# Setting the sign of the weight words with a 16-bit one-tensor operation

## The chip, the cores and the metric

The kernel runs on one core of one Trainium2 chip. The metric is the device time of one execution in microseconds; of the kernel before, three runs are given. The core's engines are TensorE (PE in the rows, its weight loads PEld), VectorE (DVE), ScalarE (ACT), GpSimd (POOL) and SyncE (SP, which issues the transfers). Each works off its own queue in order, and an instruction waits on semaphores for work of the others.

## The reference

A linear attention with an exponential feature map feeds a feed-forward layer with a squared ReLU:

```python
def phi(x):                      # q, k, v: (8, 8, 576, 64); w_phi: (64, 128)
    proj = np.einsum('bhsd,df->bhsf', x, w_phi)
    proj = proj - np.max(np.abs(proj), axis=-1, keepdims=True)
    return np.concatenate([np.exp(proj), np.exp(-proj)], axis=-1)
q_p, k_p = phi(q), phi(k)
kv, z = np.einsum('bhsf,bhsd->bhfd', k_p, v), np.sum(k_p, axis=2)
num = np.einsum('bhsf,bhfd->bhsd', q_p, kv)
x = num / (np.einsum('bhsf,bhf->bhs', q_p, z)[..., None] + 1e-06)   # to (4608, 512)
h = np.maximum(x @ w_in, 0.0)                                       # w_in: (512, 2048)
out = (h * h) @ w_out                                               # w_out: (2048, 512)
```

The two weights `w_in` and `w_out` of the feed-forward layer reach the kernel as 64-bit floats, the other inputs as 32-bit floats.

## The kernel before

**Stages.** The attention is done in 32 pairs of heads, the feed-forward layer in 18 chunks of 256 tokens by 8 blocks of 256 hidden columns. The first 6 pairs are done by the function `early`, and the weights are prepared beside them; from about 98 us on the matrix products of the feed-forward layer (lines 1180 and 1222) fill PE, with the later pairs in between.

**The weights.** Each of the two weights is cut into 8 parts of 128 x 1024 numbers; `raw0i` to `raw7i` are the parts of `w_in` and `raw0o` to `raw7o` those of `w_out`. A part comes in as 128 x 2048 32-bit words, in which low and high word of a 64-bit float alternate, so that every access to the low words or the high words has a step of 8 bytes. The function `join_words` makes 32-bit floats of them in four steps: `size` (lines 489 and 491) scales the high word, read as a 32-bit float, which brings exponent and upper fraction bits into a tile `u`; `low` (497 on ACT, 499 on DVE) rounds the low word to a number of 0 to 7 and writes it over the low word; `ends` (502, DVE) ands the sign bit out of the high word and ors it into the low word; `join` (506, DVE) shifts `u` by 3 bits and ors the low word in. Of the 16 `low` steps 13 stand on ACT and 3 on DVE. What follows on a part of `w_in` is its largest size (523), a scale (442 to 447, from PE's line 436) and the 16-bit halves `win` (565, 566, 568); on a part of `w_out` the high part `wh` (542, 544) and the rest `wl` (327, on POOL in the rows below).

**What else the prediction names.** For a pair, lines 739, 742, 749 and 752 on DVE and 745 to 757 on ACT turn the key features into exponentials; 852 and 854 do the subtraction for the queries, and 886 and 888 their exponentials; 896 on PE is the numerator. The denominator goes from PE (913) by ACT (334, tile `sx`) to a transfer (921, `den`), DVE (930, 931), a transfer to memory (934, `rd`), two transfers back that spread it over the partitions (941, `rb`), and the product on DVE (948). Line 601 and line 586 belong to the scale of the values `v`.

**What sets the order.** Each step is recorded with an estimate, its dependences and a rank; a planner puts the steps of all engines in order by a table of ranks, chooses the engine for steps that may run on two (`other=`), and the instructions are then issued in that order on each engine.

Of the kernel before, what the change touches and what calls it, by code (L numbers as in the profile page):

```python
# [16 lines left out]
BF16 = mybir.dt.bfloat16  # L17
I32 = mybir.dt.int32
U32 = mybir.dt.uint32
AF = mybir.ActivationFunctionType  # L20
ALU = mybir.AluOpType
AX = mybir.AxisListType
# [44 lines left out]
def word(x):  # L67
    return x - (1 << 32) if x >= 1 << 31 else x
# [218 lines left out]
def out_us(n):  # L287

    return 0.165 + n / 1200


def dve_us(n):
    return (n + 151) / 960
# [20 lines left out]
def tile_kernel(ctx, tc, qp, kp, vp, w_phi, w_in, w_out, out):  # L314
    nc = tc.nc
    V, A, G, PE, SP = nc.vector, nc.scalar, nc.gpsimd, nc.tensor, nc.sync
# [12 lines left out]
    def copy(n, to, of, by=None):  # L329

        if by:
            return (("ACT", out_us(n) + 0.09, lambda: A.activation(out=to(), in_=of(), func=AF.Copy, scale=by())),  # L332
                    ("DVE", dve_us(n), lambda: V.tensor_scalar(out=to(), in0=of(), scalar1=by(), scalar2=None, op0=ALU.mult), None))
        return (("ACT", out_us(n), lambda: A.activation(out=to(), in_=of(), func=AF.Copy)),
                ("DVE", dve_us(n), lambda: V.tensor_copy(out=to(), in_=of()), None))
# [129 lines left out]
    def fetch(n, f, of_in, rank):  # L465
        home = home_of[f, of_in]
        box = []
        src = w_in if of_in else w_out

        def load():  # L470
            box.append(cp.tile([128, 2048], I32, name=f"raw{f}{'io'[not of_in]}", tag=home))
            SP.dma_start(box[0], src[f])

        ld = P.add("SP", 0.47, load, [home_read[home]] if home in home_read else [], [], rank - 3.0 + 0.3 * n,
                   land=2.4, xfer=2.55)
        return ld, lambda: box[0][:, 0:2048:2], lambda: box[0][:, 1:2048:2]

    def join_words(n, f, of_in, rank):

        home = home_of[f, of_in]  # L480
        key = [("u", n)]
        u = lambda: u_[0][n]
        ld, low_w, high_w = fetch(n, f, of_in, rank)
        if of_in:
            spare[f] = low_w

        def size(E):
            if E is A:
                A.activation(out=u().bitcast(F32), in_=high_w().bitcast(F32), func=AF.Copy, scale=2.0 ** -111)
            else:  # L490
                V.tensor_scalar(out=u().bitcast(F32), in0=high_w().bitcast(F32), scalar1=2.0 ** -111, scalar2=None,
                                op0=ALU.mult)

        def low(E):
            to, of, a, b = low_w(), low_w().bitcast(U32), 0.875 * 2.0 ** -29, 0.4995
            if E is A:
                A.activation(out=to, in_=of, func=AF.Copy, scale=a, bias=b)
            else:
                E.tensor_scalar(out=to, in0=of, scalar1=a, scalar2=b, op0=ALU.mult, op1=ALU.add)

        def ends():
            V.scalar_tensor_tensor(out=low_w(), in0=high_w(), scalar=word(0x80000000), in1=low_w(),
                                   op0=ALU.bitwise_and, op1=ALU.bitwise_or)

        def join():
            V.scalar_tensor_tensor(out=u(), in0=u(), scalar=3, in1=low_w(),
                                   op0=ALU.logical_shift_left, op1=ALU.bitwise_or)

        sz = P.add("ACT", 1.15, lambda: size(A), [ld], key, rank, other=("DVE", 0.64, lambda: size(V), 4.0))
        l = P.add("ACT", 1.15, lambda: low(A), [ld], [], rank, other=("DVE", 0.68, lambda: low(V), 4.0))  # L510
        o = P.add("DVE", 1.22, ends, [l], [], rank, lock=4.0)
        o = home_read[home] = P.add("DVE", 1.22, join, [sz, o], key, rank, lock=4.0)
        return o

    def value(n, t):
        return u_[0][n].bitcast(F32).rearrange("p (t c) -> p t c", t=t)

    def split_in(n, f, rank):
        o = join_words(n, f, True, rank)
        g, i = divmod(f, 2)  # L520

        def most():
            A.activation(out=spare[f]().bitcast(F32), in_=u_[0][n].bitcast(F32), func=AF.Abs, accum_out=wmax[g][:, i:i + 1])

        most_in[f] = home_read[home_of[f, True]] = P.add("ACT", 1.06, most, [o], [("u", n)], rank)
        return o
# [9 lines left out]
    def out_high(n, f, rank, joined):  # L536
        j = slice(2 * (f % 2), 2 * (f % 2) + 2)

        def high(E):
            x = highs[f] = part(highs_of, f, F32R, "wh")[:, j]  # L540
            if E is A:
                A.activation(out=x, in_=value(n, 2), func=AF.Copy)
            else:
# [1018 lines left out]
    for n, (f, of_in) in enumerate(order_w):  # L1562
        rank = PREP0 + PREP1 * n
        if of_in:
            half[f] = n, rank, split_in(n, f, rank)
            if f % 2:
                pw = power(lambda g=f // 2: wmax[g], cw[:, f - 1:f + 1, :], TOP_W, [most_in[f - 1], most_in[f]], [],
                           half[f - 1][1], k=2)
                for x in (f - 1, f):
                    w_done[x, True] = value_in(x, *half[x], pw)  # L1570
        else:
            half_out[f] = n, f, rank, out_high(n, f, rank, join_words(n, f, False, rank))
            for x in {NFP - 2: (), NFP - 1: (f - 1, f)}.get(f, (f,)):
                w_done[x, False] = out_low(*half_out[x])
# [3 lines left out]
    for p in range(NPAIR):  # L1578
        if p % NP == 0 and p:
            b = p // NP  # L1580
# [127 lines left out]
```

## Time and profile before

| what | us |
|---|---|
| median of 3 runs (lowest, highest) | 1026.27 (1025.84, 1026.85) |
| the profiled execution, its own time | 1027.7 |
| its span, first to last instruction | 1025.9 |
| around the span | 1.8 |
| PE busy | 995.9 (97%) |
| DVE busy | 851.5 (83%) |
| ACT busy | 766.2 (75%) |
| POOL busy | 168.4 (16%) |

The span is the time from the first to the last instruction. Shares of busy time are means over stages that differ: at the start PE waits, later it hardly does. Numbers in brackets at the end of a timeline row are the engine's idle time before that group and what ended it.

### The profile page before, as it was taken

How to read it: one execution, taken by the hardware profiler on the slowest of the kernel's cores; microseconds unless marked ns; L12 is line 12 of the kernel's file. 1: busy time of each engine (PE TensorE's matmuls, PEld its weight loads, DVE VectorE, ACT ScalarE, POOL GpSimd, SP SyncE). 2: the span in 40 equal slices, each digit the busy share in tenths (PEclk: the TensorE clock that was granted, in tenths of full speed). 3: DMA queues.
4: the chain of work that ended last, by engine and by line, in shares of the span. 5: the costliest groups of instructions: out<-in, count | busy, mean ns of one | idle time of the engine just before them, and what ended most of it. 6: DMA issues, size and time to landing. Idle time of an engine off the chain costs nothing.

```text
span 1025.9 us, 21473 instructions
## 1 busy us (share of the span) xinstructions
PE 995.9 (97%) x8353; PEld 693.8 (68%) x8370; DVE 851.5 (83%) x1664; ACT 766.2 (75%) x1426; POOL 168.4 (16%) x114
## 2 busy tenths in 40 slices
PE   7887999999999999999999999999999999999998
PEld 4555676666666666566666566666666667888886
DVE  6899888898999997998888786888798899756453
ACT  7898886877989777887889667858785767654553
POOL 0013143303112112121112103102211110000000
PEclk9998999999999999999999999999999999999999
DMA  9644421221322222322323232132212111000000
GB/s 360 251 154 140 146 61 58 73 69 50 83 62 67 51 60 77 92 55 61 105 62 81 75 83 56 43 88 61 61 43 56 20 46 33 1 2 26 17 22 22
DMA packets 92937, 76.30 MB, mean 74 GB/s; under 512 B 61476, under 2 KB 70308, under 8 KB 90788
## 3 DMA queue, kind: packets, MB, share of 16 engines
q1 hardware_dynamic: 92836, 74.93, 24.8%
q8 instruction: 66, 1.08, 0.4%
q14 instruction: 35, 0.29, 0.1%
HBM read 61.18 MB, written 13.68 MB: 73 GB/s over the span
## 4 chain that ended last, share of the span: by engine, by line
PE 80%; DVE 7%; DMA 5%; ACT 4%; issue 2%; SPq 1%; POOL 0%; DVEq 0%; ACTq 0%; POOLq 0%
PE ph L1180 34%; PE po L1222 25%; PE pv L779 4%; PE pp L1495 3%; PE pn L1000 2%; DMA raw3o<-in_w_out_dram 2%; PE po L1495 2%; PE pv L1000 2%; PE pp L709 1%; PE pn L1495 1%; PE pv L1495 1%; PE pp L1076 1%; PE pv L784 1%; DMA raw0i<-in_w_in_dram 1%; DMA rb<-rd 1%
## 5 line engine op out<-in xcount | busy, mean ns | idle before, releaser
L1180 PE MATMUL ph<-ring,win 128*128 128x256 f16 x3456 | 392.5, 273 | 1.2 <-DVE gl L327 1.2
L1180 PEld LDWEIGHTS <-win 128*128 128x128 f16 x3456 | 334.9, 98 | 61.3 <-issue 13.3
L1222 PE MATMUL po<-wl,gh 128*128 128x512 f16 (+1 forms) x767 | 185.4, 379 | 1.4 <-issue 0.8
L1099 POOL PARTITION_ALL_REDUCE mx<-pt x52 | 116.3, 2237 | 426.7 <-ACT pt L332 274.5
L1222 PEld LDWEIGHTS <-gh 128*128 128x128 f16 (+1 forms) x784 | 75.0, 98 | 83.3 <-issue 5.1
L327 DVE TENSOR_TENSOR gl<-ph,gh 128x512 f16<-128x512 f32 (+1 forms) x114 | 77.5, 680 | 21.9 <-ACT ph L1201 15.1
L1222 PE MATMUL po<-wl,gl 128*128 128x512 f16 x328 | 84.3, 379 | 0.0
L1197 ACT ACTIVATE r<-ph,cwr 128x512 f32<-128x512 f32 x82 | 55.8, 682 | 36.8 <-PE ph L1180 36.3
L1222 PEld LDWEIGHTS <-gl 128*128 128x128 f16 (+1 forms) x456 | 41.9, 98 | 55.8 <-issue 7.4
L1199 ACT ACTIVATE gh<-r 128x512 f16<-128x512 f32 (+1 forms) x114 | 71.3, 625 | 5.1 <-PE pv L1495 3.0
L779 PE MATMUL pv<-e,v 128*64 128x256 f32 x512 | 64.7, 389 | 6.0 <-ACT e L747 4.2
L327 DVE TENSOR_TENSOR v<-qe,gh 128x896 f16<-128x896 f32 x30 | 32.8, 1092 | 42.3 <-ACT gh L1483 42.0
L1201 ACT ACTIVATE ph<-r 128x512 f32<-128x512 f32 x114 | 67.2, 590 | 0.3
L779 PEld LDWEIGHTS pv<-e,v 128*64 128x64 f32 x512 | 36.3, 140 | 23.9 <-ACT e L747 6.1
L1104 ACT ACTIVATE qe<-qe 128x576 f32<-128x576 f32 x52 | 35.3, 679 | 20.1 <-DVE qe L327 19.7
L327 DVE TENSOR_TENSOR qe<-pt,mx 128x576 f32<-128x576 f32 x52 | 39.7, 764 | 10.4 <-POOL mx L1099 10.3
L1115 DVE SCALAR_TENSOR_TENSOR pt<-qe,zc,pt 128x576 f32<-128x576 f32 x52 | 41.9, 810 | 5.4 <-ACT pt L1111 5.2
L1483 ACT ACTIVATE gh<-qe 128x896 f16<-128x896 f32 x30 | 28.4, 946 | 24.0 <-PE pv L1495 8.8
L1495 PEld LDWEIGHTS <-gh 128*128 128x128 f16 x420 | 41.1, 98 | 4.7
L1468 ACT ACTIVATE r<-ph,cwr 128x512 f32<-128x512 f32 x30 | 20.6, 686 | 29.4 <-PE ph L1180 29.3
L1477 DVE TENSOR_TENSOR qe<-qe 128x256 f32<-128x256 f32 (+1 forms) x90 | 28.8, 375 | 15.9 <-ACT qe L1473 15.8
L745 ACT ACTIVATE e<-e,sc 128x512 f32<-128x512 f32 x48 | 34.2, 716 | 9.0 <-DVE e L742 8.7
(369 smaller groups left out, 1983.1 us busy)
## 6 DMA issues: line engine op xcount, KB each, us to landing
v<-in_vp_dram SPq DMA_DIRECT2D x32, 320.0 KB
k<-in_kp_dram SPq DMA_DIRECT2D x32, 288.0 KB
q<-in_qp_dram SPq DMA_DIRECT2D x32, 288.0 KB
rb<-rd SPq DMA_DIRECT2D x64, 144.0 KB
out_dram<-o SPq DMA_DIRECT2D x28, 256.0 KB
td<-kvs SPq DMA_DIRECT2D x26, 128.0 KB
kz<-td SPq DMA_DIRECT2D x104, 32.0 KB
zq<-zd SPq DMA_DIRECT2D x104, 2.0 KB
```

The costliest lines, as they stand in the source:

```text
L327: eng.tensor_tensor(out=out_, in0=a, in1=b_, op=ALU.subtract)
L779: PE.matmul(out=to[64 * h:64 * h + 64, 0:256], lhsT=v_[p][:, t, h, :], rhs=e_[2 * p + h][:, t].rearrange("p s f -> p (s f)"), start=t == 0 ...
L1000: PE.matmul(out=to[64 * h:64 * h + 64, :], lhsT=kz_[n][:, 128 * s_ + 64 * h:128 * s_ + 64 * h + 64], rhs=qe_[2 * n + h].rearrange("p (s x) ...
L1099: o = P.add("POOL", par_us(S), lambda n=n, h=h: G.partition_all_reduce(mx_[n], pt_[p][:, h, :], channels=128, reduce_op=bass_isa.ReduceOp. ...
L1104: o = P.add("ACT", act_us(S), lambda qe=qe: A.activation(out=qe(1), in_=qe(0), func=AF.Exp, scale=-1.0), [o], [("qe", n)], R(RQ + 0.4))
L1115: o = P.add("DVE", dve_us(S) + 0.05, lambda h=h, qe=qe, y=y: V.scalar_tensor_tensor(out=y(), in0=qe(1), scalar=zc_[p][:, 2 * h + 1:2 * h + ...
L1180: PE.matmul(out=ph[:, j, :], lhsT=win[w][:, t, 128 * ff:128 * ff + 128], rhs=ring[half][x][:, t, c0:c0 + T], start=k == 0, stop=k == 3 * K ...
L1197: o = P.add("ACT", act_us(512, 1), lambda: A.activation(out=r_[n], in_=ph_[bank], func=AF.Relu, scale=by()), [g1] + wait, [("ph", bank), ( ...
L1199: sq = P.add("ACT", act_us(512), lambda: A.activation(out=gh(), in_=r_[n], func=AF.Square), [o], [("r", n), ("gh", n)], Q)
L1201: o = P.add("ACT", 0.59, lambda: A.activation(out=ph_[bank], in_=r_[n], func=AF.Square), [o], [("ph", bank), ("r", n)], Q, other=("DVE", 0 ...
L1222: PE.matmul(out=po_[po[i][1]], lhsT=g[:, j, 128 * i:128 * i + 128], rhs=w[:, j, :], start=(f == (NFP - ENDS if last else 0) and (s, j) == ...
L1495: PE.matmul(out=to, lhsT=l()[:, a], rhs=r(slice(b_, b_ + 1))[:, 0], start=(f == 0 and k == 0 and place % 2 == 0), stop=(f == NFP - 1 - END ...
```

## The change

`ends` becomes an operation on one tensor. It no longer reads the low word: it reads the upper 16 bits of the high word, ands them with 0x8000 and writes the result to the upper 16 bits of the low word. So that this leaves a clean word, `low` writes its number of 0 to 7 as a 16-bit integer to the lower 16 bits of the low word alone; it still reads all 32 bits. Both 16-bit accesses have a step of 8 bytes, as the 32-bit ones had. `join` reads the same 32-bit word as before.

```diff
+U16 = mybir.dt.uint16
...
+        halves = lambda x: x().bitcast(U16)
+
         def low(E):
-            to, of, a, b = low_w(), low_w().bitcast(U32), 0.875 * 2.0 ** -29, 0.4995
+            to, of, a, b = halves(low_w)[:, :, 0], low_w().bitcast(U32), 0.875 * 2.0 ** -29, 0.4995
             if E is A:
                 A.activation(out=to, in_=of, func=AF.Copy, scale=a, bias=b)
             else:
                 E.tensor_scalar(out=to, in0=of, scalar1=a, scalar2=b, op0=ALU.mult, op1=ALU.add)
 
         def ends():
-            V.scalar_tensor_tensor(out=low_w(), in0=high_w(), scalar=word(0x80000000), in1=low_w(),
-                                   op0=ALU.bitwise_and, op1=ALU.bitwise_or)
+            V.tensor_scalar(out=halves(low_w)[:, :, 1], in0=halves(high_w)[:, :, 1], scalar1=0x8000, scalar2=None,
+                            op0=ALU.bitwise_and)
```

The planner's estimates, ranks and dependences are untouched. On every engine the same instructions stand in the same order as before; 16 of them on DVE are of another kind (TENSOR_SCALAR in place of SCALAR_TENSOR_TENSOR), and 16 `low` instructions have another output. `ends` still waits for `low` of its part. Two parts, `raw5i` and `raw4o`, swap the buffers of `u` that they get, so that of the two `size` instructions on ACT that stand next to each other (at 80.3 and 81.3 us) the second now waits for POOL's `wl` and the first for DVE, where it was the other way round; and the load of `raw6o` waits, besides what it waited for, for ACT's `low` of the part that lay in its buffer before.

## Rows read from the trace of the kernel before

**Rows 1.** The page's parts 1 and 2: the span, busy time by engine, and the granted TensorE clock in 40 equal slices (in tenths of full speed).

```profile
span 1025.9 us, 21473 instructions
...
PE 995.9 (97%) x8353; PEld 693.8 (68%) x8370; DVE 851.5 (83%) x1664; ACT 766.2 (75%) x1426; POOL 168.4 (16%) x114
...
PEclk9998999999999999999999999999999999999999
```

**Rows 2.** Busy time by stretch of the span. Columns: stretch, its length, busy us (and instructions) of PE, PEld, DVE, ACT and POOL, granted clock, share of the transfer engines, GB/s.

```profile
58.00:69.00 11.00, 9.47 (x121) 5.83 (x120) 10.77 (x16) 10.68 (x21) 2.38 (x1) 1.00 0.63 230
69.00:82.00 13.00, 8.48 (x111) 5.69 (x105) 12.59 (x20) 12.35 (x19) 3.17 (x1) 0.91 0.33 96
82.00:98.00 16.00, 13.27 (x125) 8.13 (x125) 13.55 (x20) 12.45 (x22) 5.04 (x2) 0.75 0.52 179
98.00:140.00 42.00, 40.96 (x344) 29.23 (x339) 36.63 (x63) 35.42 (x60) 7.28 (x3) 1.00 0.34 113
140.00:1026.00 886.00, 877.13 (x7178) 614.18 (x7191) 732.57 (x1461) 648.12 (x1221) 147.48 (x101) 1.00 0.21 55
```

**Rows 3.** What PE waited for from 98 us to the end: us in total, times, longest us. The three largest.

```profile
PE pp L1076 <- DVE e L742: 1.4, 2, 1.0
PE ph L1180 <- DVE gl L327: 1.2, 1, 1.2
PE pp L877 <- ACT qe L888: 0.9, 1, 0.9
```

**Rows 4.** The instructions of line 502 (`ends`, the first and the last of 16) and of line 499 (`low` on DVE, the first and the last of 3): ns min/median/max, first and last start in us, shape.

```profile
L502 DVE SCALAR_TENSOR_TENSOR raw0i<-raw0i x1: 1210/1210/1210, 17.6 to 17.6; 128x1024 int32<-128x1024 int32 x1
...
L502 DVE SCALAR_TENSOR_TENSOR raw7o<-raw7o x1: 1216/1216/1216, 132.7 to 132.7; 128x1024 int32<-128x1024 int32 x1
...
L499 DVE TENSOR_SCALAR raw0i<-raw0i x1: 687/687/687, 14.4 to 14.4; 128x1024 int32<-128x1024 uint32 x1
...
L499 DVE TENSOR_SCALAR raw7i<-raw7i x1: 705/705/705, 117.4 to 117.4; 128x1024 int32<-128x1024 uint32 x1
```

**Rows 5.** Timelines up to 47 us: ACT (its step before the transfer `den`, and the step that waits for it), SP's issue of that transfer, and two waits of DVE. Columns: start us, us, engine, line, operation, out<-in, shape, count, and in brackets the idle time before.

```profile
32.51 0.53 ACT L334 ACTIVATE sx<-pn 128x288 f32<-128x288 f32 x1
...
39.67 0.74 ACT L586 ACTIVATE sx<-v 128x640 bf16<-128x640 f32 x1 [3.49 <-DMA den<-sx]
...
33.34 0.70 SPq L921 DMA_DIRECT2D den<-sx  x1
...
43.83 1.23 DVE L502 SCALAR_TENSOR_TENSOR raw0o<-raw0o 128x1024 int32<-128x1024 int32 x1 [1.64 <-ACT raw0o L497]
...
46.27 0.29 DVE L852 TENSOR_REDUCE qm<-pn 128x1 f32<-128x128 f32 x1 [0.61 <-PE pn L847]
```

**Rows 6.** Timelines of 68 to 82 us, with the columns of rows 5: ACT, PE, DVE, POOL and SP, in this order.

```profile
68.00 1.22 ACT L497 ACTIVATE raw2o<-raw2o 128x1024 int32<-128x1024 uint32 x1
...
72.40 2.19 ACT L565 ACTIVATE win<-u,cw 128x1024 f16<-128x1024 f32 x2
...
70.17 0.71 PE L436 MATMUL pn<-ident,wm 128*128 128x128 f32 x4
...
81.26 2.19 PE L896 MATMUL pn<-qe,kz 128*64 128x288 f32 x8 [1.30 <-DVE pt L854]
...
69.24 1.23 DVE L502 SCALAR_TENSOR_TENSOR raw2o<-raw2o 128x1024 int32<-128x1024 int32 x1 [0.48 <-ACT raw2o L497]
...
70.99 0.41 DVE L442 TENSOR_REDUCE pw<-pn 128x2 f32<-128x256 f32 x1
...
72.84 1.19 DVE L502 SCALAR_TENSOR_TENSOR raw4o<-raw4o 128x1024 int32<-128x1024 int32 x1
...
75.09 1.27 DVE L568 SCALAR_TENSOR_TENSOR win<-u,cw,win 128x1024 f16<-128x1024 f32 x1
...
76.48 1.27 DVE L568 SCALAR_TENSOR_TENSOR win<-u,cw,win 128x1024 f16<-128x1024 f32 x1
77.68 2.36 DVE L930 TENSOR_SCALAR den<-den 128x9 f32<-128x9 f32 x1
...
80.20 0.71 DVE L948 TENSOR_TENSOR rb<-n,rb 128x576 f32<-128x576 f32 x1
80.83 0.28 DVE L854 TENSOR_TENSOR pt<-pn,qm 128x128 f32<-128x128 f32 x1
...
76.83 3.17 POOL L327 TENSOR_TENSOR wl<-u,wh 128x1024 bf16<-128x1024 f32 x1 [9.16 <-ACT wh L542]
...
76.14 1.30 SPq L941 DMA_DIRECT2D rb<-rd  x2
```

**Rows 7.** The chain of waits, a piece of an earlier pair: start us, us from issue to landing of the second of its two `rb` transfers.

```profile
52.92 4.48 DMA rb<-rd
```

**Rows 8.** Busy time by stretch, with the columns of rows 2, around PE's half-speed stretches.

```profile
79.50:80.00 0.50, 0.45 (x8) 0.20 (x4) 0.50 (x1) 0.50 (x2) 0.50 (x1) 0.72 0.00 0
80.00:81.20 1.20, 0.00 (x0) 0.00 (x0) 1.17 (x5) 1.20 (x3) 0.01 (x1) 0.50 0.03 2
81.20:85.80 4.60, 4.54 (x20) 2.49 (x20) 3.57 (x5) 4.28 (x9) 0.00 (x0) 0.50 0.24 70
85.80:89.40 3.60, 0.88 (x8) 0.58 (x8) 3.57 (x6) 3.15 (x8) 0.00 (x0) 0.90 0.37 98
90.00:93.40 3.40, 3.40 (x22) 2.01 (x22) 3.38 (x3) 2.52 (x5) 2.66 (x1) 0.50 0.71 267
```

## The prediction, made before the changed kernel was run

> **What bounds the kernel now.** I read the page's busy times and clock first. PE is busy for 995.9 of 1025.9 us, and the granted clock is at or near full speed in all 40 slices but one tenth in the first [rows 1]. Of the 30 us in which PE is not busy most must lie early, so I cut the span into stretches [rows 2]. From 98 us on PE is busy for 40.96 of 42.00 and then for 877.13 of 886.00 us at a granted clock of 1.00. Before that it is not: 9.47 of 11, 8.48 of 13, 13.27 of 16, at granted clocks of 1.00, 0.91 and 0.75. There DVE and ACT are both nearly full (10.77 and 10.68 of 11, 12.59 and 12.35 of 13). So the end is set by how early the preparation lets PE's solid run begin, and after 98 us almost by PE alone: its three largest sums of waits come to 1.4 + 1.2 + 0.9 = 3.5 us, and none of them names a weight word of `ends` or `low` [rows 3]. Only then did I read timelines, at each place where DVE or ACT had been waiting, to see whose end came last there [rows 5, 6].
>
> **What the change removes.** An `ends` takes 1.210 us at first and 1.216 at last; the nearest one-tensor operation of DVE, on the same 1024 numbers with the same step of 8 bytes, is `low`, with 0.687 and 0.705 [rows 4]. I take 0.68 for the new `ends`, a gain of 0.53 each, 16 x 0.53 = 8.5 us of DVE. The bounds: 1.21, no gain, if the engine gives the 16-bit access no more than two tensors get; and, on the low side, half of the 0.69, if a 16-bit element goes at twice the pace of a 32-bit one.
>
> The Trainium skill ("VectorE: DVE Perf Modes", "What auto-detection actually checks") has a rule for this: twofold speed for one source in SBUF with fitting dimensions, and fourfold only if every tensor is also 16-bit with step 1. The step here is 4 elements, so by the page `ends` would get the twofold speed, as the `low` of rows 4 seems to (0.69 against 1.21), and not the fourfold; by fourfold the sum below would hardly change, because it is not the size of the gain that limits it.
>
> `low` keeps its instruction and writes 2 bytes instead of 4. On ACT it takes 1.22 us (at 68.00), and the two `win` instructions, which write 16 bits, take 2.19 / 2 = 1.10 each for as many numbers [rows 6]. So I take no change, with bounds of -0.1 and, upward, the 0.6 of a rival below. The order stays on all engines; the swapped `u` buffers and the added wait of a load I cost at nothing, because ACT's two `size` instructions stand next to each other, and a load is asked for long after its buffer's `low`. If that cover were gone, ACT would stand up to one step of about 1.2 us.
>
> **Where the gain goes.** I follow 0.53 us down each stretch.
> - The early parts, up to 39.67 us: ACT runs without a gap to its step `sx` at 32.51, which ends at 33.04; the transfer `den` is issued at 33.34, and ACT then stands for 3.49 us until it has landed [rows 5]. What DVE gains before that adds to this wait and moves nothing: 0.
> - `raw0o` at 43.83: DVE stood 1.64 us for ACT's `low` before it, and 0.61 after it for PE's line 847 at 46.27 [rows 5]. The gain goes into the second wait: 0. The parts after it up to 69 us end in front of the next one, where DVE already stands 0.48 us for ACT's `low` of `raw2o` (68.00 + 1.22 = 69.22; `ends` begins at 69.24) [rows 6], while ACT has been busy for 10.68 of 11 us [rows 2]. What DVE gains is added to the 0.48: 0.
> - `raw2o` at 69.24: it would end 0.53 earlier, but the follower that counts is line 442 at 70.99, which needs PE's line 436, ending at 70.17 + 0.71 = 70.88. Gain there at most 70.99 - 70.88 = 0.11.
> - `raw4o` at 72.84: begins 0.11 earlier and is 0.53 shorter, 0.64 in all. The next limit is line 568 at 75.09, which needs ACT's pair of `win`, ending at 72.40 + 2.19 = 74.59: so 0.50 at most passes. The second 568 then starts at 75.98 and ends at about 77.25. POOL's `wl` is recorded from 76.83 for 3.17 us, to 80.00, and `den` (line 930), 128 x 9 numbers, is recorded for 2.36 us, to 80.04: it ends with `wl` [rows 6]. I read this as the two engines keeping each other out: `den` waits for `wl`, and `wl` for the second 568, which ended at 76.48 + 1.27 = 77.75. If 568 ends 0.5 earlier, so do `wl` and `den`, and DVE's line 948 could begin at 79.7 instead of 80.20. But it needs the spread denominator `rb`, whose two issues run from 76.14 to 77.44, the second from 76.14 + 0.65 = 76.79; an earlier pair took 4.48 us from issue to landing [rows 7], which would be 81.3, too late for 80.20, so this one was quicker; and in the half microsecond before 80.00 no byte moves [rows 8], so it had landed by about 79.5 at the earliest reading, or the record of its end is late. I take 0.1 of the 0.5, and keep 0 and 0.5 as bounds.
> - PE's line 896 at 81.26 had waited 1.30 us for DVE's line 854 (80.83 + 0.28 = 81.11), which follows 948 at once [rows 6]. So the 0.1 reaches PE. The stretches behind it, 81.2 to 85.8 and 90.0 to 93.4, are granted 0.50, that is 1.2 GHz, with PE busy for 4.54 and 3.40 us [rows 8]; work that comes in 0.1 earlier in the second at full speed before it gives another 0.1 or 0.2.
> - From 98 us on: PE has 1.04 us of slack in 42 [rows 2], of which `ends` ends none [rows 3]: 0, at most some tenths.
>
> Sum: 0.1 + 0.2 = 0.3 us. The profiled execution took 1027.7 (1025.9 and 1.8 around it), so it would take 1027.4; that lies 1.4 above the median of the runs, as far as before, since nothing in the time around the span is touched. On the median: 1026.27 - 0.3 = 1026.0.
>
> **The rivals.**
> 1. *DVE's saving reaches the end.* If DVE were the bound of the preparation, 16 x 0.53 = 8.5 us would come off: 1017.7; if a quarter of it passed, 1024.1. For it speaks that DVE is busiest before 82 us [rows 2]; against it that at every place followed above something else (`den`, PE's 847 and 436, ACT's `low` and `win`) ends within 0 to 0.5 us of DVE [rows 5, 6].
> 2. *The half-speed stretches shrink.* PE fell to 0.50 after it had stood in 80.0 to 81.2 and again after it had been busy for only 0.88 of 3.60 us in 85.8 to 89.4 [rows 8]. If the shift lets PE keep 2.4 GHz in the second, its 3.40 us of work would take 1.70: 1.5 off in round numbers, 1026.27 - 0.2 - 1.5 = 1024.6; with both stretches (4.54 / 2 = 2.27 more) 1022.3. For it: a few tenths decide where the clock falls. Against it: the gap of 80 to 81.2 that goes before becomes 0.1 shorter at most.
> 3. *It doesn't do what it says.* The 16-bit access with a step costs what two tensors do, 1.2 us. Then nothing moves: 1026.2.
> 4. *Slower: the 16-bit halves are dear to write.* `low` then writes 2 of every 8 bytes, and no row shows this. If it cost ACT half as much again, 1.22 x 0.5 = 0.6 each, ACT would be the bound where DVE already waits for it: at `raw0o` (43.83), `raw2o` (69.24) and behind `win` (74.59) [rows 5, 6], 3 x 0.6 = 1.8, and the four or five `low` that stand before 32.51 would bring `den` later by some 0.6 of what is not covered. 1026.27 + 2.4 = 1028.7. It decides from about 0.5 us on each `low`; at 0.3 it is 1.2, to be counted as no change. Against it: `win`, which writes 16 bits, is no longer on ACT.
>
> On this last one the Trainium skill ("SBUF — State Buffer", "Door 1: The DMA port swizzle (why `[64,N]` ≈ `[32,N]`)", note on cachelines) says that accesses go at full speed as long as two of them fall into one 16-byte line. The 8-byte step gives two in a line before and after, so by the page the price would be nothing and the sum as it stands; no run so far shows it.
>
> **How the numbers follow.** About 0.2%, 2.05 us, is what a measurement of this kernel can tell from no change; so faster means under 1024.2 and slower over 1028.3. The forecast has 0.53 (own range 1025.3 to 1026.9, from the bounds 0 and 0.5 of the one passage, a few tenths elsewhere and the spread of the runs). Rival 1 has 0.10, all of it faster. Rival 2 has 0.14, of which 0.05, both stretches, is faster. Rival 3 has 0.11, rival 4 0.12, counted as slower. Faster 0.10 + 0.05 = 0.15; slower 0.12; same 0.73. For 8 in 10 the range reaches down to rival 2 with some of rival 1, 1023.8, and up close to rival 4, 1028.2.
>
> **What would show it.** Line 502's successor at 0.65 to 0.75 us, 16 times, and `low` on ACT as before (1.22 for `raw2o`); DVE's wait for ACT's `low` of `raw2o` grown from 0.48 to 1 us or more; line 442 at most 0.1 earlier; 948 between 79.7 and 80.2; PE's busy time from 98 us on unchanged. The forecast is wrong if PE's solid run begins over 2 us earlier or later, if the stretch from 90 us is granted full speed, or if `low` on ACT has grown by half a microsecond.

## The result and the profile after

The changed kernel takes 1035.75 us (median of 5 runs, 1035.09 to 1037.6) where the kernel before takes 1026.27 (1025.84 to 1027.28): a ratio of 1.0094, with a 95% interval of 1.008 to 1.0109. It is 9.5 us slower; the forecast was 1026.0, with a range up to 1028.2. The profiled execution took 1037.6 and is the longest of the five.

The page of the changed kernel, parts 1 and 2, the lines that answer to [rows 1]:

```profile
span 1035.8 us, 21474 instructions
...
PE 1003.0 (97%) x8353; PEld 695.7 (67%) x8370; DVE 853.0 (82%) x1664; ACT 781.1 (75%) x1426; POOL 168.0 (16%) x114
...
PEclk8897999999999999999999999999999999999999
```

DVE was to lose 8.5 us of work and has gained 1.5; ACT, with as many instructions as before, has 14.9 us more. The instructions themselves show why. These are the groups of the changed kernel's lines 505 (`ends`), 500 (`low` on ACT) and 502 (`low` on DVE), the first and the last of each; columns as in [rows 4]:

```profile
L505 DVE TENSOR_SCALAR raw0i<-raw0i x1: 1339/1339/1339, 20.1 to 20.1; 128x1024 uint16<-128x1024 uint16 x1
...
L505 DVE TENSOR_SCALAR raw7o<-raw7o x1: 1342/1342/1342, 143.8 to 143.8; 128x1024 uint16<-128x1024 uint16 x1
...
L500 ACT ACTIVATE raw1i<-raw1i x1: 2472/2472/2472, 20.9 to 20.9; 128x1024 uint16<-128x1024 uint32 x1
...
L500 ACT ACTIVATE raw7o<-raw7o x1: 2483/2483/2483, 141.3 to 141.3; 128x1024 uint16<-128x1024 uint32 x1
...
L502 DVE TENSOR_SCALAR raw0i<-raw0i x1: 1317/1317/1317, 14.6 to 14.6; 128x1024 uint16<-128x1024 uint32 x1
...
L502 DVE TENSOR_SCALAR raw7i<-raw7i x1: 1341/1341/1341, 128.1 to 128.1; 128x1024 uint16<-128x1024 uint32 x1
```

All three kinds of instruction that write 16 bits at a step of 8 bytes take about twice what the like instruction took with words. `low` on ACT went from 1.19 to 2.51 us (means of its 13), `low` on DVE from 0.69 to 1.33 [rows 4], and `ends`, as a one-tensor operation expected at 0.68, takes 1.34, more than the 1.23 of the two-tensor operation that it replaced (medians of the 16). ACT's 13 x 1.32 = 17.2 us are by far the largest item.

ACT's timeline in the changed kernel, up to 50 us, as in [rows 5]:

```profile
20.89 2.47 ACT L500 ACTIVATE raw1i<-raw1i 128x1024 uint16<-128x1024 uint32 x1
...
40.84 0.42 ACT L335 ACTIVATE sx<-pn 128x288 f32<-128x288 f32 x1
41.13 2.55 ACT L500 ACTIVATE raw5i<-raw5i 128x1024 uint16<-128x1024 uint32 x1
...
44.02 2.48 ACT L500 ACTIVATE raw3o<-raw3o 128x1024 uint16<-128x1024 uint32 x1
...
46.85 0.75 ACT L589 ACTIVATE sx<-v 128x640 bf16<-128x640 f32 x1
...
49.84 2.50 ACT L500 ACTIVATE raw0o<-raw0o 128x1024 uint16<-128x1024 uint32 x1
```

The reader is to see two things. The step `sx<-v` begins at 46.85 and has no bracket: the 3.49 us that ACT stood for `den` at 39.67 in the kernel before [rows 5] are gone, and it comes 7.2 us later all the same. Not all of the 7.2 is the change's: in this execution the first `ends` already began 2.5 us late (20.05 against 17.6 [rows 4]), after a start at half clock that the last section describes. The rest is near 6 x 1.32 - 3.49 = 4.4, the six `low` before this step less the wait that they used up. And from 41 to 80 us ACT doesn't stand at all, as the stretches of the changed kernel say (columns as in [rows 2]; ACT's is the fourth number after the length, 19.00 of 19 and 20.00 of 20):

```profile
41.00:60.00 19.00, 15.00 (x183) 10.62 (x181) 15.90 (x29) 19.00 (x27) 0.00 (x0) 0.91 0.28 74
60.00:80.00 20.00, 17.40 (x198) 10.62 (x200) 18.15 (x27) 20.00 (x37) 4.75 (x2) 1.00 0.50 175
...
150.00:1035.00 885.00, 877.72 (x7188) 613.86 (x7200) 732.95 (x1463) 648.32 (x1223) 148.52 (x101) 1.00 0.21 55
```

From 150 us on PE is busy for 877.72 of 885 us at full speed, as it was from 140 us on before (877.13 of 886 [rows 2]): all of the loss is in front. On DVE's `ends` it can be followed: that of `raw2o` begins at 78.04 (69.24 before [rows 6], 8.8 later), 2.5 of it from the same start, and before it DVE waits for ACT, by the waits of the changed kernel:

```profile
DVE raw2o L505 <- ACT raw2o L500: 1.8, 1, 1.8
DVE raw0o L505 <- ACT raw0o L500: 1.7, 1, 1.7
```

The forecast had the wait at `raw2o` grow from 0.48 to 1 us because DVE would come earlier. It grew because ACT came later. At `raw0o` it stayed as it was (1.64 before [rows 5]). The two `size` instructions on ACT whose buffers of `u` are swapped still run back to back (89.36 and 90.38 us), so the swap shows no cost. The span is 9.9 us longer than that of the profile before, 0.4 more than the medians differ by.

### The profile page after: what moved, and what is told of

The parts are those of the page before. It is cut to its first block, busy times and chain, and to the rows that moved or that the text cites. A ratio compares the mean times of both kernels' runs of the same rounds, so it can differ in the third digit from the quotient of the medians.

```text
span 1035.8 us, 21474 instructions
## 1 busy us (share of the span) xinstructions
PE 1003.0 (97%) x8353; PEld 695.7 (67%) x8370; DVE 853.0 (82%) x1664; ACT 781.1 (75%) x1426; POOL 168.0 (16%) x114
## 4 chain that ended last, share of the span: by engine, by line
PE 81%; ACT 5%; DVE 4%; DMA 1%; issue 1%; POOL 0%; SPq 0%; DVEq 0%; ACTq 0%; POOLq 0%
PE ph L1183 33%; PE po L1225 26%; PE pv L782 4%; PE pp L1498 3%; PE pn L1003 2%; PE pv L1003 2%; PE po L1498 2%; PE pp L712 2%; PE pn L1498 1%; PE pp L1079 1%; PE pv L1498 1%; PE pv L787 1%; PE pn L1079 1%; PE pn L725 1%; ACT r L1200 0%
## 5 line engine op out<-in xcount | busy, mean ns | idle before, releaser
L328 DVE TENSOR_TENSOR v<-qe,gh 128x896 f16<-128x896 f32 x30 | 32.8, 1092 | 42.3 <-ACT gh L1486 42.0
L782 PEld LDWEIGHTS pv<-e,v 128*64 128x64 f32 x512 | 35.9, 144 | 23.9 <-issue 4.6
L1107 ACT ACTIVATE qe<-qe 128x576 f32<-128x576 f32 x52 | 35.2, 678 | 20.6 <-DVE qe L328 20.5
L1471 ACT ACTIVATE r<-ph,cwr 128x512 f32<-128x512 f32 x30 | 20.6, 685 | 29.5 <-PE ph L1183 29.3
L1225 PE MATMUL po<-wh,gh 128*128 128x512 f32 x128 | 40.9, 441 | 0.0
```

Source lines behind the costliest of these rows:

```text
L328: eng.tensor_tensor(out=out_, in0=a, in1=b_, op=ALU.subtract)
L782: PE.matmul(out=to[64 * h:64 * h + 64, 0:256], lhsT=v_[p][:, t, h, :], rhs=e_[2 * p + h][:, t].rearrange("p s f -> p (s f)"), start=t == 0 ...
L1107: o = P.add("ACT", act_us(S), lambda qe=qe: A.activation(out=qe(1), in_=qe(0), func=AF.Exp, scale=-1.0), [o], [("qe", n)], R(RQ + 0.4))
L1225: PE.matmul(out=po_[po[i][1]], lhsT=g[:, j, 128 * i:128 * i + 128], rhs=w[:, j, :], start=(f == (NFP - ENDS if last else 0) and (s, j) == ...
```

## The experiments

Times are medians, each beside the kernel before on the same chip: 1027.35 us for the first three, 1027.41 for the next three with a time, 1026.51 for the last two.

**`ends` alone.** The change without its edit of `low`:

```diff
-            to, of, a, b = halves(low_w)[:, :, 0], low_w().bitcast(U32), 0.875 * 2.0 ** -29, 0.4995
+            to, of, a, b = low_w(), low_w().bitcast(U32), 0.875 * 2.0 ** -29, 0.4995
```

> `ends` as in the change (one tensor, 16-bit), `low` as before (32-bit words). Theory A, the loss comes from `low`, which writes halves in 2.5 us on ACT where it wrote words in 1.2: `ends` stays at 1.34 us, 0.12 over before, DVE's extra 16 x 0.12 = 1.9 us is mostly hidden as in my prediction, and the time is 1026 to 1028 us. Theory B, the 16-bit `ends` has a large part in the loss, by waits that it adds on DVE: 1029 us or more.

Measured: 1026.4 us, ratio 0.9997 (0.9983 to 1.001). One `ends` of this kernel:

```profile
L505 DVE TENSOR_SCALAR raw7o<-raw7o x1: 1333/1333/1333, 134.9 to 134.9; 128x1024 uint16<-128x1024 uint16 x1
```

The 16-bit `ends` costs its 0.11 us more each here too, and nothing of it can be told at the end (-1.7 to +1.0 us). Theory A holds: the loss hangs on the edit of `low`.

**The gain that was meant, without a 16-bit write.**

```diff
-            V.scalar_tensor_tensor(out=low_w(), in0=high_w(), scalar=word(0x80000000), in1=low_w(),
-                                   op0=ALU.bitwise_and, op1=ALU.bitwise_or)
+            V.tensor_scalar(out=low_w(), in0=high_w(), scalar1=word(0x80000000), scalar2=None, op0=ALU.bitwise_and)
```

> Before, with `ends` as a one-tensor operation on whole 32-bit words; it writes the sign alone over the low word, so that the three lowest bits of each weight are left out of the computation. This is the gain on DVE that I had forecast, without a 16-bit write. `ends` should take about 0.69 us. If the gain is swallowed by other waits, as the prediction had it: 1025.3 to 1026.9 us. If DVE's saving reaches the end (rival 1): near 1017.7, and under 1024.1 already for a quarter of it.

Measured: 1027.46 us, ratio 0.9995 (0.998 to 1.001). The last of its `ends`, and its step `sx<-v` on ACT:

```profile
L502 DVE TENSOR_SCALAR raw7o<-raw7o x1: 684/684/684, 132.8 to 132.8; 128x1024 int32<-128x1024 int32 x1
```

```profile
39.98 0.74 ACT L585 ACTIVATE sx<-v 128x640 bf16<-128x640 f32 x1 [1.13 <-issue]
```

`ends` takes 0.67 to 0.74 us 15 times (and 1.43 once, for `raw5i`, which took 2.05 before), as I had put in, and the time doesn't move (-2.1 to +1.0 us). So the second half of the prediction, that other waits swallow 8.5 us of DVE, was right; its median lies 0.6 over my own range for this, because the kernel before ran 1.1 longer on this chip than in the runs I started from. Rival 1, that DVE's saving reaches the end, falls. One of the places can be seen: DVE's wait for ACT before the `ends` of `raw2o`, 0.48 us in the kernel before [rows 6], has grown as the forecast said:

```profile
DVE raw2o L502 <- ACT raw2o L497: 1.8, 1, 1.8
```

The step `sx<-v` begins at 39.98, at the same time as before; I come back to that.

**The same time on ACT without a 16-bit write.**

```diff
                 A.activation(out=to, in_=of, func=AF.Copy, scale=a, bias=b)
+                A.activation(out=to, in_=of, func=AF.Copy, scale=a, bias=b)
```

> Before, with each of the 13 `low` on ACT done twice in a row on 32-bit words; the second pass makes the number 0, so that the three lowest bits of these weights are left out. ACT then has about 2.3 us at each `low`, as in the changed kernel (2.5), and no 16-bit access anywhere. If ACT's time at `low` is the whole cause of the loss: 1033 to 1036 us. If the 16-bit writes cost something besides their own time (other engines' accesses, the longer `ends` and `low` on DVE): 1030 us or less.

Measured: 1035.07 us, ratio 1.0074 (1.0051 to 1.0097), 7.7 us slower. One of the second passes:

```profile
L498 ACT ACTIVATE raw3i<-raw3i x1: 1151/1151/1151, 25.2 to 25.2; 128x1024 int32<-128x1024 uint32 x1
```

Thirteen passes more of some 1.15 us, 15 us, cost in much the same proportion what 17.2 cost in the changed kernel (7.7 / 15 = 0.51; 9.5 / 17.2 = 0.55). ACT's time alone, without a 16-bit access anywhere, brings a loss of this size. Nothing else about the 16-bit writes, such as a hold on other engines, is needed; with an interval of 5.2 to 10.0 us a small share of something else, such as the three longer `low` on DVE, can't be ruled out.

**Early and late `low`.** The change, with halves written by the first nine parts only (against the changed kernel), and then by the last seven only (against the first of the two):

```diff
             to, of, a, b = halves(low_w)[:, :, 0], low_w().bitcast(U32), 0.875 * 2.0 ** -29, 0.4995
+            if (f, of_in) not in {(1, True), (3, True), (4, True), (2, True), (5, True), (3, False), (0, False), (0, True), (1, False)}:
+                to = low_w()
```

> The change, with the 16-bit `low` only in the first nine parts (seven on ACT, two on DVE, all begun before 53 us in the changed kernel); the other seven write words. The theory is that the loss is ACT's time in the stretch up to about 43 us, where ACT has no gap: six `low` with 1.32 us more each are 7.9, less the 1.8 us that ACT stands there otherwise. So 5.5 to 7 us of the 9.5 should stay: 1031.5 to 1034. If every `low` on ACT counted alike, 7 of 13 would leave 5.1: 1031.4. If the early ones were absorbed in the waits for transfers, as the prediction had it, under 1029.

```diff
-            if (f, of_in) not in {(1, True), (3, True), (4, True), (2, True), (5, True), (3, False), (0, False), (0, True), (1, False)}:
+            if (f, of_in) in {(1, True), (3, True), (4, True), (2, True), (5, True), (3, False), (0, False), (0, True), (1, False)}:
```

> The change, with the 16-bit `low` only in the last seven parts (six on ACT, one on DVE, from 75 us on in the changed kernel). By the theory of the early stretch the rest of the loss is here: 2 to 3.5 us, so 1028.5 to 1030.5. If every `low` counted alike, 6 of 13 would give 4.4: 1031. If `low` under PE's solid run cost nothing and only the two at 75 to 81 us count: 1027 to 1028.5.

Measured: the early ones 1033.31 us, ratio 1.0053 (1.0036 to 1.007), 5.9 us slower; the late ones 1030.17, ratio 1.0022 (1.0005 to 1.004), 2.8 us slower. Together 8.7 of 9.5. Both lie where the theory of the early stretch had them, but the theory had counted six `low` and a wait of 1.8 us; with the seven early `low` and the 3.49 of [rows 5] it gives 7 x 1.32 - 3.5 = 5.7, which fits as well. The seven early `low` on ACT cost 0.84 us each and the six late ones 0.46. Neither is free, but the intervals (3.7 to 7.2 and 0.5 to 4.1 us) hardly exclude that every `low` counts alike (5.1 and 4.4 us). The traces say more. With the early halves ACT's step `sx<-v` begins 4.4 us later than before (39.67 [rows 5]), with the first `ends` only 0.5 later (18.14):

```profile
44.05 0.82 ACT L591 ACTIVATE sx<-v 128x640 bf16<-128x640 f32 x1
```

With the late halves ACT works on `raw5o` until 102.3 us, and PE then waits for ACT's `qe`, which comes behind it on ACT with other steps in between (the like wait was 0.9 us before [rows 3]):

```profile
PE pp L882 <- ACT qe L893: 2.8, 1, 2.8
```

**No `low` at all.** On top of the fast `ends`:

```diff
         def low(E):
-            to, of, a, b = low_w(), low_w().bitcast(U32), 0.875 * 2.0 ** -29, 0.4995
-            if E is A:
-                A.activation(out=to, in_=of, func=AF.Copy, scale=a, bias=b)
-            else:
-                E.tensor_scalar(out=to, in0=of, scalar1=a, scalar2=b, op0=ALU.mult, op1=ALU.add)
+            pass
```

> As e2_fast_ends, and `low` issues no instruction at all; the three lowest bits of each weight are left out. ACT loses 13 x 1.16 = 15 us, DVE 3 x 0.69 = 2 us more. If ACT is the engine that bounds the preparation, the time falls about as far as twice the `low` raised it: 1019 to 1022 us. If other things end last as soon as ACT is quicker (transfers, PE, DVE), it stays at 1024 or more.

Measured: 1025.94 us, ratio 0.9988 (0.997 to 1.0006): no difference that can be told. This was a miss, and the most instructive one: 15 us more on ACT cost 7.7, and 15 us less (with some 10 less on DVE) give back nothing measurable. ACT's step `sx<-v` in this kernel, and its stretches around 40 us (columns as in [rows 2], the share of the transfer engines is the last but one):

```profile
40.40 0.74 ACT L581 ACTIVATE sx<-v 128x640 bf16<-128x640 f32 x1 [5.66 <-DMA den<-sx]
```

```profile
36.00:38.00 2.00, 1.91 (x27) 1.75 (x29) 2.00 (x5) 0.00 (x0) 0.00 (x0) 1.00 0.97 378
38.00:40.00 2.00, 1.70 (x26) 0.82 (x22) 2.00 (x5) 0.00 (x0) 0.00 (x0) 1.00 0.63 217
40.00:42.00 2.00, 0.00 (x0) 0.00 (x0) 1.72 (x6) 1.60 (x4) 0.00 (x0) 0.89 0.08 14
```

There is a gate at 40 us. ACT has nothing to do from 36 to 40 us and waits 5.66 us for `den`, which lands when the transfer engines fall idle, and not before. In the kernel before the wait was 3.49, to 39.67 [rows 5]; with the fast `ends` the step began at 39.98. Less work in front of the gate only lengthens the wait; more work fills the wait first (3.5 us) and then moves everything behind it. That explains the asymmetry for the early `low`. Why the savings behind the gate (seven `low`, and `ends`) give nothing either isn't settled by this run.

**The gate.** The first `den` issued by ACT, once in the kernel before and once in the kernel without `low`:

```diff
-        o = P.add("SP", 0.65, lambda: SP.dma_start(
+        o = P.add("SP", 0.65, lambda: (A if p == 0 else SP).dma_start(
```

> Before, with the first pair's transfer `den` issued by ACT instead of SP, so that it doesn't stand in SP's queue behind the loads of the weights; nothing else. It tests the gate at 40 us: in before and in the kernels with less work on ACT and DVE, ACT stood until this transfer had landed at 39.7 to 40.4 us, however early it was issued. If SP's full queue holds it, it lands at 36 to 38 us and ACT's wait falls from 3.5 to under 2 us. If the gate alone keeps the preparation from ending earlier, the time falls by as much, to 1024 to 1025.5 against before; if the places behind it swallow the gain, as in the prediction's steps, it stays within 0.2%. If the transfer engines themselves hold it, it lands at 39.5 as before.

> e7_no_low (no `low` at all, `ends` on whole words, three lowest bits of each weight left out) with the first `den` issued by ACT. There ACT stood 5.7 us for `den`. If the gate at 40 us is what swallowed the 15 us taken from ACT in e7_no_low, this one falls by 2.5 us or more against e7_no_low, to 1020 to 1023.5. If other waits behind it are in line, it stays at 1025 to 1027.

Measured: 1028.24 us, ratio 1.0021 (1.0008 to 1.0033), and 1025.12, ratio 0.999 (0.9978 to 1.0001). ACT's timeline in the first of them:

```profile
33.15 1.10 ACTq L921 DMA_DIRECT2D den<-sx  x1
...
40.16 0.74 ACT L586 ACTIVATE sx<-v 128x640 bf16<-128x640 f32 x1 [3.64 <-DMA den<-sx]
```

Issued by another engine, with no load ahead of it in that queue, the transfer lets ACT go on at 40.16, as before, and at 39.57 in the kernel without `low`. So it isn't SP's queue that holds it. Over seven kernels the step begins between 39.57 and 40.40 us, wherever in 32.8 to 35.9 us `den` was issued (in three of them, the fast `ends` among them, the profile names nothing that ended the wait); that fits transfer engines which are fully taken by the loads until about 39 us, but no run took loads away, so that remains a reading. As the gate didn't move, these two runs don't say what opening it would bring. The 1.7 us by which the first is slower aren't explained; ACT's issue alone takes 1.10 us.

**What a 16-bit write costs.** A program of its own with single accesses, each three times in a row:

```diff
+    s = src.bitcast(U32)[:, 0:2 * N:2]
+    d = {"words": ta["words"][:, 0:2 * N:2], "halves": ta["halves"].bitcast(U16)[:, 0:4 * N:4],
+         "upper": ta["upper"].bitcast(U16)[:, 1:4 * N:4], "every": ta["every"].bitcast(U16)[:, 0:2 * N:2],
+         "sparse": ta["sparse"].bitcast(U16)[:, 0:8 * N:8], "wide": ta["wide"][:, 0:4 * N:4],
...
+        A.activation(out=d["halves"], in_=s, func=AF.Copy, scale=a, bias=b)
+        V.tensor_scalar(out=d["halves"], in0=s, scalar1=a, scalar2=b, op0=ALU.mult, op1=ALU.add)
```

> A program of its own, which computes nothing of the reference: each form of access three times on ACT, then on DVE, 1024 elements a partition, the form of `low` unless said. Theory P, a write of half a word alone goes at half pace, whatever the step: 16 bits at steps of 4, 8 and 16 bytes 2.4 us on ACT and 1.3 on DVE; packed 16 bits, pairs of 16 bits that fill a word, and whole words at any step up to 16 bytes 1.2 and 0.7. Theory S, the step decides, counted in elements: 16 bits at a 4-byte step (2 elements, as the words of `low`) 1.2 and 0.7, and 32-bit words at a 16-byte step (4 elements) slow as the halves are. Theory R, the 16-bit read is dear: reading halves at a step of 8 bytes and writing words 2.4 and 1.3.

Groups of this program, ACT and then DVE: line, engine, operation, out<-in, shapes, count, and behind the bar the busy us in all and the mean ns of one. `words`, `wide` and `wider` are 32-bit words at 8, 16 and 32 bytes; `every`, `halves` and `sparse` are 16 bits at 4, 8 and 16 bytes, `upper` as `halves`; `packed` is 16 bits without gaps, `pairs` two times 16 bits that fill one word in 8 bytes; `rword` reads 16 bits at 8 bytes and writes words.

```profile
L72 ACT ACTIVATE sparse<-src 128x1024 uint16<-128x1024 uint32 x3 | 14.2, 4747 | 0.1
...
L51 ACT ACTIVATE halves<-src 128x1024 uint16<-128x1024 uint32 x3 | 7.4, 2456 | 1.0 <-DVE halves L33 1.0
L69 ACT ACTIVATE wider<-src 128x1024 int32<-128x1024 uint32 x3 | 6.1, 2040 | 0.1
L66 ACT ACTIVATE wide<-src 128x1024 int32<-128x1024 uint32 x3 | 6.1, 2036 | 0.1
L57 ACT ACTIVATE every<-src 128x1024 uint16<-128x1024 uint32 x3 | 4.2, 1396 | 0.0
L75 ACT ACTIVATE rword<-src 128x1024 int32<-128x1024 uint16 x3 | 3.7, 1219 | 0.0
L48 ACT ACTIVATE words<-src 128x1024 int32<-128x1024 uint32 x3 | 3.4, 1150 | 3.7 <-DVE words L33 3.7
L81 ACT ACTIVATE pairs<-src 128x1024 uint16<-128x1024 uint32 x3 | 3.4, 1137 | 0.0
...
L60 ACT ACTIVATE packed<-src 128x1024 uint16<-128x1024 uint32 x3 | 3.3, 1104 | 0.0
```

```profile
L93 DVE TENSOR_SCALAR sparse<-src 128x1024 uint16<-128x1024 uint32 x3 | 7.4, 2467 | 19.4 <-ACT sparse L72 19.4
...
L114 DVE TENSOR_SCALAR halves<-src 128x1024 uint16<-128x1024 uint32 x3 | 4.1, 1350 | 0.0
...
L121 DVE TENSOR_SCALAR upper<-src 128x1024 uint16<-128x1024 uint16 x3 | 3.9, 1301 | 0.0
...
L99 DVE TENSOR_SCALAR wide<-src 128x1024 int32<-128x1024 uint32 x3 | 3.2, 1069 | 0.0
L90 DVE TENSOR_SCALAR rword<-src 128x1024 int32<-128x1024 uint16 x3 | 2.5, 841 | 1.6 <-ACT rword L75 1.6
L117 DVE TENSOR_SCALAR words<-src 128x1024 int32<-128x1024 uint32 x3 | 2.2, 742 | 0.0
L108 DVE TENSOR_SCALAR every<-src 128x1024 uint16<-128x1024 uint32 x3 | 2.2, 739 | 0.0
```

None of the three theories holds whole. The read isn't it: `rword` costs 1.22 against 1.15 us on ACT. Half words as such aren't it: at 4 bytes 16 bits take 1.40 on ACT and 0.74 on DVE, near to words. The step in elements isn't it: 4 elements are 2.46 us for `halves` and 2.04 for `wide`, but 8 are 4.75 for `sparse` and 2.04 for `wider`. What fits is the number of 16-byte pieces that are written, at a price that is over twice as high if parts of words are written in them. `halves` writes into 512 such pieces, `sparse` into 1024 (4.8 and 4.6 ns a piece on ACT), `wide` into 1024 (2.0 ns). `every` writes into 256, at 1.40 us a little more than the 1.2 that this price gives. A second program was to test that:

> A program of its own, which computes nothing of the reference: more forms of access, three times on ACT, then on DVE. Theory L, what costs is each 16-byte line that is written, about 2 ns on ACT if only whole words are written in it (the 32-bit words at 16 and 32 bytes took 2.0 us), about 4.7 if parts of words are (16 bits at 16 bytes took 4.7, at 8 bytes 2.5): 16 bits at 32 bytes then take 4.7 us on ACT and 2.5 on DVE as at 16 bytes, pairs of 16 bits that fill one word in every 16 bytes 1.1 to 1.3 and 0.7, single bytes at a step of 8 bytes 2.5 and 1.35, at 4 bytes 1.4 and 0.74. Theory E, the step in elements decides: 16 bits at 32 bytes (16 elements) 9 us and 5, bytes at 8 bytes (8 elements) 4.7 and 2.5, at 4 bytes 2.5 and 1.35. Reading at steps of 16 or 32 bytes and writing densely: as dear as the same writes (2.0 and 1.07 us) if a line costs in both directions.

Its groups, with `sparser` for 16 bits at 32 bytes, `bytes` and `bytefew` for single bytes at 8 and 4 bytes, `farpair` for a pair that fills one word in 16 bytes, and `rwide` for a read of words at 16 bytes:

```profile
L61 ACT ACTIVATE sparser<-src 128x1024 uint16<-128x1024 uint32 x3 | 13.6, 4534 | 1.1 <-DVE sparser L33 1.1
...
L67 ACT ACTIVATE bytes<-src 128x1024 uint8<-128x1024 uint32 x3 | 7.3, 2444 | 0.0
...
L76 ACT ACTIVATE rwide<-src 128x1024 int32<-128x1024 uint32 x3 | 6.3, 2085 | 0.0
...
L70 ACT ACTIVATE bytefew<-src 128x1024 uint8<-128x1024 uint32 x3 | 4.1, 1371 | 0.0
L64 ACT ACTIVATE farpair<-src 128x1024 uint16<-128x1024 uint32 x3 | 3.6, 1203 | 0.0
```

```profile
L106 DVE TENSOR_SCALAR sparser<-src 128x1024 uint16<-128x1024 uint32 x3 | 7.4, 2451 | 0.0
...
L100 DVE TENSOR_SCALAR bytes<-src 128x1024 uint8<-128x1024 uint32 x3 | 3.9, 1310 | 15.2 <-ACT bytes L67 15.2
```

Theory L holds in all of its figures here but one: bytes at 4 bytes take 0.86 us on DVE where 0.74 was said, and packed ones no less (0.89), so that this belongs to bytes. At 32 bytes a half word costs what it costs at 16 (4.53 and 4.75), a byte at 8 bytes what a half word costs there, and a pair that fills its word is cheap at 16 bytes (1.20). What the memory does inside is not shown by this; the rule of thumb is.

## Why the prediction was wrong

- **`low` keeps its length** ("I take no change, with bounds of -0.1 and, upward, the 0.6"). This is the step that failed. The prediction's sum had nothing for this term; it measured +1.32 us on each of 13 `low` on ACT and +0.64 on each of 3 on DVE. The row that I leaned on, `win` with 1.10 us, also writes 16 bits, but without gaps: `packed` at 1.10 and `halves` at 2.46 show how far such a row is from the case. The nearest row must agree in the thing that changes, here in how much of each word is left standing between two writes.
- **`ends` gains 0.53.** It lost 0.11 (1.34 for 1.23). The bounds that I gave, 1.21 at most, excluded it. With words, the one-tensor form takes 0.68 as I had said. By itself this miss moved no time that can be told.
- **Two rules of the Trainium skill.** The Trainium skill's rule on modes ("VectorE: DVE Perf Modes", "What auto-detection actually checks") would give twofold speed to `ends`, and the trace has 1.34 us where the word form has 0.68. The Trainium skill's note on cachelines ("SBUF — State Buffer", "Door 1: The DMA port swizzle (why `[64,N]` ≈ `[32,N]`)") would let two accesses in a 16-byte line go free: words at 8 bytes bear that out (1.15 us on ACT against 2.04 at 16 bytes), half words don't (2.46 with two in a line). The measurement decides.
- **Rival 4, dear halves on `low`,** was the right mechanism at half its price: 0.6 us against 1.32. Its places were wrong too. It took three `low` as on the path and most of those before 33 us as covered. ACT had no gap there, so each of the six before its step `sx<-v` counted, less the 3.5 us that `den` had made ACT wait. I had read that ACT runs without a gap to `sx` for the question what DVE's gain is worth; read for the other side, the same row says that every microsecond more on ACT there counts as soon as the wait behind it is used up. Priced at 1.32 and with `raw0o`, which follows, it gives 5.7 us for the early parts, where halves measured 5.9; this count was made after the results.
- **Other waits swallow DVE's gain.** Right within what the runs can tell: with `ends` at 0.68 the time is the same (0.998 to 1.001). The 0.3 us of the sum is too small to be seen, and of its places only the wait at `raw2o` was read again.
- **From 98 us on nothing is lost.** For DVE's gain this stood; for ACT it was too simple. The six late `low` cost 2.8 us, and behind one of them PE waits 1.9 us longer than before (2.8 for 0.9).
- **Rival 2, shorter half-speed stretches,** can't be read from the changed kernel, since everything was moved. Its reading of the rows was off: the granted clock was at 0.72 from 79.5 to 80.0 us and at 0.50 from 80.0 on [rows 8], so PE's standing from 80.0 to 81.2 can't have brought it down. **Rival 3,** a 16-bit access that costs what two tensors do, is nearly what `ends` did; it left `low` out.

No version here beats the kernel before: the fast `ends` and even the kernel without any `low` run level with it.

## What to carry to other kernels

Before narrowing a write, count the 16-byte pieces that it touches and ask if it leaves parts of words standing: 16 bits at a step of 8 bytes doubled the time on both engines, while the same 16 bits without gaps or in pairs that fill a word cost nothing. A merge of two fields by partial writes is therefore no free replacement for a bitwise operation of two tensors. And slack is one-sided: ACT, which runs without a gap up to its wait for a transfer, gained nothing there by less work, and by more work lost what exceeded that wait, so a slower case must be priced with its own count of places, not with that of the gain.

## What was unexpected on the hardware

In the two programs of single accesses, bytes and half words written alone at 8 bytes or more cost by the 16-byte piece, 4.4 to 4.8 ns a piece on ACT and 2.4 to 2.7 on DVE, against 2.0 and 1.05 for whole words; and reads at 16 bytes are about as dear as writes of words there (`rwide` 2.09 us on ACT, `wide` 2.04). The granted clock of PE early in the span also differs between executions of kernels whose order on PE is the same. From 11.8 to 18.8 us it was 1.00 (2.4 GHz) in the kernel before and 0.51 (nearly all of it at 1.2 GHz) in the changed one, where no changed instruction ran until 14.6. From 10 to 12 us, ahead of the fall, PE had been busy for 0.61 us in the changed kernel and for 0.76 in the one before:

```profile
11.80:18.80 7.00, 5.49 (x72) 3.46 (x72) 4.60 (x12) 6.60 (x14) 0.00 (x0) 1.00 1.02 420
```

```profile
11.80:18.80 7.00, 5.88 (x22) 3.16 (x23) 3.38 (x6) 4.51 (x10) 0.00 (x0) 0.51 1.02 424
```

The later the first `ends`, the lower was this clock: over the profiles it began at 17.6 to 17.8 us at 1.00, at 18.1 at 0.93, at 19.0 to 19.5 at 0.76 and at 20.1 to 20.8 at 0.51 to 0.60. In the kernel with the fast `ends` (0.60, first `ends` at 20.6) the wait at 40 us took this up, and the step `sx<-v` began at 39.98; the changed kernel has no such wait left, so that there the late start comes on top of the longer `low`. How much of the 9.5 us between the medians it makes up isn't known, since only one execution of each kernel has a trace, and the profiled times don't settle it: with the 16-bit `ends` alone (0.59) the execution took 3.1 us more than its median though the step began at 40.29, and with `low` twice (0.53), where the wait is used up as well, it lay 0.1 under its median.
